# Threshold attention with a SoLU layer behind it: k and q two pairs to a transfer, w_out's copies two pieces at a time, four tiles' swaps issued by GpSimd

## The chip, the core and the metric

The kernel runs on one core of a Trainium2 chip. The core has five engines that run on their own and meet at semaphores: TensorE (PE in the profile, with PEld for its weight loads), VectorE (DVE), ScalarE (ACT), GpSimd (POOL) and SyncE (SP). Transfers are issued by an engine's queue (SPq, ACTq, or GpSimd's) and carried out by 16 DMA engines. The metric is the device time of one execution in microseconds (us); lower is better. Every engine works through its own instructions in order, so an instruction that waits holds all that stand behind it on that engine.

## What is computed

```python
scores = scale * np.matmul(q, k.transpose(0, 1, 3, 2))      # 8 batches, 8 heads, 576 x 576
thresh = np.max(scores, axis=-1, keepdims=True) - tau
scores = np.where(scores >= thresh, scores, -1000000000.0)
attn = np.exp(scores - np.max(scores, axis=-1, keepdims=True))
attn = attn / (np.sum(attn, axis=-1, keepdims=True) + 1e-09)
x = np.matmul(attn, v)                                       # then (B,H,S,D) -> (B*S, H*D)
h = x @ w_in                                                 # 4608 x 512 @ 512 x 1024
e = np.exp(h - h_max)
solu = h * (e / (np.sum(e, axis=-1, keepdims=True) + 1e-09))
ln = (solu - mu) / np.sqrt(var + 1e-06) * g_ln
out = ln @ w_out                                             # 1024 x 512
```

The head dimension is 64, so two heads (a pair) lie beside each other on the 128 partitions. A batch has 4 pairs and 576 tokens.

## The kernel before

**Rounds.** The order of all work is written out by hand. A loop over `rnd` takes one slot (128 score rows of each head of a pair, or left-over rows) per round. A round puts on TensorE the scores of the slot (`scores`, L399) with any transposes of later k and q that are due (`turn_beside`, L344), then a quarter of a feed-forward tile (`ff_h`, L560 and L570, or `ff_o`, L675) or the product with v of an earlier slot (`attend_steps`, L507) or both. VectorE finds each row's threshold (`maxes`, L420), ScalarE applies it and takes exponentials (`ramp` L435, `exps` L444), GpSimd divides by the sums one round later (`normalise`, L451 to L454), and VectorE transposes the result into T (`blocks`, L466).

**T to wT.** After every second slot `blocks` issues on SyncE the copies that regroup T into wT (L475 and L477, three transfers; L482, four, for the left-over rows). L507 needs wT. This is half of all bytes moved.

**Loads of k and q.** Batch 0 comes pair by pair, 128 rows at a time (`load_pair`, L133). Batch 1 comes two pairs at a time (`load_four`, L135 to L142), for k and q of pairs 4 and 5 in rounds 10 and 11, of pairs 6 and 7 in rounds 15 and 16. It puts head e of pair i and head e of pair i + 1 on the two halves of one tile, and issues each half as a transfer of its own, so a call issues four. L344 reads both tiles of a call. Later batches are loaded in another way (`load_natural`, L168) and are transposed by VectorE (L186), with copies of the halves (L188).

**Weights.** w_in and w_out come in 16 pieces of 128 x 512 words of 64 bits, each loaded by SyncE (`weight_load`, L248) and turned into 32 bits by VectorE, ScalarE and GpSimd over two rounds (`weight_e`, `weight_m`, `weight_b`, L258 to L295; `weight_c`, L305). Pieces 8 to 15 are w_out's. For each of them `weight_d` issues two transfers that copy its halves, exchanged, into the odd slots of w2 (L312). `ff_o` reads w2's slots in order, the first eight in its first quarter, and does not run before round and piece counts say that w2 is complete.

**The feed-forward tile.** After `ff_h` a tile's 128 tokens go through `ff_max` (L585), `ff_exp` (L594), `ff_mul` (L600), `ff_sum` (L605), `ff_stats` (L615 to L626), each a round or so apart. Then ScalarE writes the normalised values into V (`ff_norm`, L636), VectorE writes them into u (`ff_norm2`, L641), and `ff_swap` issues four transfers that overwrite quarters of V by rows of u (L652), which exchanges halves. `ff_turn` transposes V into uT (L662), which `ff_o` needs. `ff_norm2` and `ff_swap` stand in the part of the round that the program calls `middle`: behind `normalise` and `weight_c`, ahead of the round's TensorE work in the program's order. Tiles have names of three numbers (batch, kind, m) or one number (the left-over rows of two batches); batch 0 has four of three numbers.

**Queues.** All transfers but two (the first k and half of the last store) are issued by SyncE, in the order of the program.

Of the kernel before, what the change touches and what calls it, by code (L numbers as in the profile page):

```python
# [20 lines left out]
def kernel(  # L21
# [27 lines left out]
    nc = tc.nc  # L49
# [10 lines left out]
    ROWS = (slice(0, 64), slice(64, P))  # L60
# [10 lines left out]
    w2 = const.tile([P, 2 * NC, DM], F32, name="w2")  # L71
# [63 lines left out]
    def load_four(i, nm):  # L135
        heads_of = rows_of[nm][P * i : P * i + 2 * P].rearrange("(j e p) n -> e j p n", j=2, e=2)
        for e in range(2):
            tag = "ends" if nm == "q" and i > NP else nm
            raw = loads.tile([P, NK * D], F32, tag=tag, bufs=BUFS[tag], name=nm)
            whole_rows[i, nm, e] = raw.rearrange("p (m d) -> p m d", m=NK)  # L140
            for j in range(2):
                nc.sync.dma_start(out=raw[ROWS[j]], in_=heads_of[e, j])  # L142

    def load_v(b, hf, parts):
        d = halves.setdefault((b, hf), {})
# [161 lines left out]

    def weight_d(x):
        c = x - 2 * NP
        if c >= 0:  # L310
            for r in range(2):
                nc.sync.dma_start(out=w2[ROWS[r], 2 * c + 1], in_=w2[ROWS[1 - r], 2 * c])  # L312

# [233 lines left out]
    def ff_h(t, part, split, beside=()):  # L549
        beside = iter(beside)  # L550
        x = tokens(t)
        if part == 0:
            tag, h = take("h_ps")
            ffn[t] = dict(h=h, tag=tag, split=split)
        d = ffn[t]
        h = d["h"]
        if not d["split"]:
            f = slice(512 * part, 512 * part + 512)
            for c in range(NP):
                nc.tensor.matmul(  # L560
                    out=h[:, f], lhsT=x[:, c], rhs=w1_parts[:, c, part],
                    start=c == 0, stop=c == NP - 1,
                )
            return
        last = []
        for c in range(NP):
            for r in range(2):
                f = slice(512 * (part ^ r), 512 * (part ^ r) + 512)
                for y in range(2):
                    mm = nc.tensor.matmul(  # L570
                        out=h[ROWS[y], f], lhsT=x[ROWS[r], c, ROWS[y]], rhs=w1_parts[ROWS[r], c, part ^ r],
                        start=part == 0 and c == 0, stop=part == 1 and c == NP - 1,
                    )
                    if part and not last:
                        sync(mm, d["fence"])
                    last.append(mm)
            for _, _ in zip(range(36 * (c > 1)), beside):
                pass
        if part == 0:
            d["fence"] = fence(last[-4:])  # L580

    def ff_max(t):
        d = ffn[t]
        d["nm"] = small.tile([P, 1], F32, tag="hm", name="hm")
        nc.vector.tensor_reduce(out=d["nm"], in_=d["h"], axis=AX.X, op=ALU.max, negate=True)  # L585

    def ff_exp(t):
        d = ffn[t]

        starts.append(t)  # L590
        tag = "xh1" if rnd > NS and len(starts) % 2 else "u"
        d["u"] = work.tile([P, DFF], F32, tag=tag, bufs=1, name="u")
        d["se"] = small.tile([P, 1], F32, tag="se", name="se")
        nc.scalar.activation(  # L594
            out=d["u"], in_=d["h"], func=AF.Exp, bias=d["nm"], scale=1.0, accum_out=d["se"]
        )

    def ff_mul(t):
        d = ffn[t]
        nc.vector.tensor_tensor(out=d["u"], in0=d["h"], in1=d["u"], op=ALU.mult)  # L600
        pairs_free.append(d["tag"])

    def ff_sum(t):
        se = ffn[t]["se"]
        nc.gpsimd.tensor_scalar(out=se, in0=se, scalar1=1e-9, scalar2=None, op0=ALU.add)  # L605
        nc.gpsimd.tensor_tensor(out=se, in0=se, in1=mone[:, 0:1], op=ALU.pow)

    def ff_stats(t):
        d = ffn[t]
        u, se = d["u"], d["se"]  # L610
        bs = small.tile([P, 2, 6], F32, tag="bs", name="bs")
        mv = small.tile([P, 2], F32, tag="mv", name="mv")
        rs = small.tile([P, 1], F32, tag="rs", name="rs")
        for f in range(2):
            nc.vector.bn_stats(out=bs[:, f], in_=u[:, 512 * f : 512 * f + 512])  # L615
        nc.vector.bn_aggr(out=mv, in_=bs)


        nc.gpsimd.tensor_scalar(
            out=rs, in0=mv[:, 1:2], scalar1=se, scalar2=se, op0=ALU.mult, op1=ALU.mult  # L620
        )
        nc.gpsimd.tensor_scalar(out=rs, in0=rs, scalar1=1e-6, scalar2=None, op0=ALU.add)
        nc.gpsimd.tensor_tensor(out=rs, in0=rs, in1=mhalf, op=ALU.pow)
        nc.gpsimd.tensor_tensor(out=rs, in0=rs, in1=se, op=ALU.mult)
        nb = small.tile([P, 1], F32, tag="nb", name="nb")
        nc.gpsimd.tensor_scalar(  # L626
            out=nb, in0=mv[:, 0:1], scalar1=rs, scalar2=-1.0, op0=ALU.mult, op1=ALU.mult
        )
        d["norm"] = rs, nb

    def ff_norm(t):
        d = ffn[t]
        rs, nb = d["norm"]
        d["V"] = V = work.tile([P, 2, DFF // 2], F32, tag="V", bufs=1, name="V")
        u = d["u"].rearrange("p (g n) -> p g n", g=2)
        nc.scalar.activation(out=V, in_=u, func=AF.Identity, bias=nb, scale=rs)  # L636

    def ff_norm2(t):
        d = ffn[t]
        rs, nb = d["norm"]  # L640
        nc.vector.tensor_scalar(  # L641
            out=d["u"], in0=d["u"], scalar1=rs, scalar2=nb, op0=ALU.mult, op1=ALU.add
        )

    def ff_swap(t):
        d = ffn[t]
        for g in range(2):
            for r in range(2):  # L650
                to, of = 64 * r + 32 * g, 64 * r + 32 * (1 - g)
                nc.sync.dma_start(  # L652
                    out=d["V"][to : to + 32, 1 - g],
                    in_=d["u"][of : of + 32, DFF // 2 * g : DFF // 2 * g + DFF // 2],
                )
# [118 lines left out]
    with tc.manual_schedule():  # L774
# [44 lines left out]
        begin, middle, late, norms = {}, {}, {}, {}  # L819
        while True:  # L820
# [10 lines left out]
            if rnd == NS:  # L831
# [4 lines left out]
                if quarter == 2:  # L836
                    between.append(cur)
                    cur = None
                    quarter = 0
                assert quarter != 3  # L840
            if rnd == 13:
                prev, cur, quarter = cur, None, 0
            if (
# [3 lines left out]
                cur = ready[0][1].pop(0)  # L847
# [60 lines left out]
            if step == ("h", 0):  # L908
                ff_h(cur, 0, rnd + 1 < NS, beside)
                quarter = 1  # L910
            elif step == ("h", 1):
                ff_h(cur, 1, None, beside)
                quarter = 2
                by = rnd + 2 * (rnd == 14)
                late.setdefault(by, []).append(lambda t=cur: (ff_max(t), ff_exp(t)))
                late.setdefault(by + 1, []).append(lambda t=cur: (ff_mul(t), ff_sum(t)))
                middle.setdefault(by + 2, []).append(lambda t=cur: ff_stats(t))
                if rnd + 6 < NS:
                    norms[by + 3] = cur
                else:  # L920
                    late.setdefault(rnd + 2, []).append(lambda t=cur: ff_norm(t))
                middle.setdefault(by + 3, []).append(lambda t=cur: (ff_norm2(t), ff_swap(t)))

                at = by + 4 if more or not ready or len(ready[0][1][0]) == 1 else rnd + 6
                if cur == (0, 1, 1):
                    middle.setdefault(rnd + 6, []).append(lambda t=cur, at=rnd + 6: ff_turn(t, at))
                else:
                    late.setdefault(at, []).append(lambda t=cur, at=at: ff_turn(t, at))
                if not more:
                    between.append(cur)  # L930
                    cur = None
                    quarter = 0
            elif step == ("o", 0):
                if prev is not None:
                    ff_o(prev, 0)
                quarter = 3
            elif step == ("o", 1):
                if prev is not None:
                    ff_o(prev, 1)
                    last = not (more or ready or cur or between)  # L940
                    begin.setdefault(rnd + 1, []).append(lambda t=prev, last=last: ff_out(t, last))
                    late.setdefault(rnd + 1, []).append(lambda t=prev, last=last: ff_store(t, last))
                prev, cur = cur, None
                quarter = 0
# [33 lines left out]
            if rnd - 1 in pieces:  # L978
                weight_d(pieces[rnd - 1])
                w2_done = pieces[rnd - 1] == NW - 1  # L980
# [36 lines left out]
```

## Time and profile before

| What | Value |
|---|---|
| Median of 3 runs | 858.18 us (855.24 to 861.62) |
| Profiled execution | 855.96 us |
| Its span, first to last instruction | 854.2 us |
| PE busy | 819.7 us, 96% |
| DVE busy | 680.4 us, 80% |
| ACT busy | 572.3 us, 67% |
| POOL busy | 499.1 us, 58% |
| SyncE's DMA queue | 165.82 MB, packets 77.3% of 16 engines' span |
| Chain that ended last | PE 80%, DVE 7%, DMA 6%, ACT 3% |
| Transfers T to wT | 160 of 288 KB and 64 of 576 KB |
| Swaps V from u | 144 of 64 KB, median 3.4 us to landing |

A group's row in the profile has its source line (L675 is line 675), the engine, the operation, the tile written and the tile read, the number of instructions and their time. In square brackets stand idle time ahead of an instruction and what ended it. A transfer's row on SPq is the time that SyncE needs to issue it; the transfer itself goes on behind that, and the trace records at what time each DMA engine reports its part as landed.

### The profile page before, as it was taken

How to read it: one execution, taken by the hardware profiler on the slowest of the kernel's cores; microseconds unless marked ns; L12 is line 12 of the kernel's file. 1: busy time of each engine (PE TensorE's matmuls, PEld its weight loads, DVE VectorE, ACT ScalarE, POOL GpSimd, SP SyncE). 2: the span in 40 equal slices, each digit the busy share in tenths (PEclk: the TensorE clock that was granted, in tenths of full speed). 3: DMA queues.
4: the chain of work that ended last, by engine and by line, in shares of the span. 5: the costliest groups of instructions: out<-in, count | busy, mean ns of one | idle time of the engine just before them, and what ended most of it. 6: DMA issues, size and time to landing. Idle time of an engine off the chain costs nothing.

```text
span 854.2 us, 36120 instructions
## 1 busy us (share of the span) xinstructions
PE 819.7 (96%) x15363; PEld 613.4 (72%) x15363; DVE 680.4 (80%) x1241; ACT 572.3 (67%) x1127; POOL 499.1 (58%) x945
## 2 busy tenths in 40 slices
PE   6679889999999999999999999999999999999997
PEld 5456666667677787777688877777777777777655
DVE  6999868889788888888788878888888888787361
ACT  6888857877666666666676667766667777775121
POOL 3888637666556656565566666565666655555120
PEclk8889999999999999999999999999999999999999
DMA  9989897898889788887889787888888887655212
GB/s 339 265 236 231 208 206 185 227 250 208 225 208 227 194 191 205 219 214 181 216 212 220 194 177 200 212 212 212 200 207 228 202 195 188 154 136 140 67 39 63
DMA packets 75442, 168.54 MB, mean 197 GB/s; under 512 B 11274, under 2 KB 32786, under 8 KB 75282
## 3 DMA queue, kind: packets, MB, share of 16 engines
q1 hardware_dynamic: 74994, 165.82, 77.3%
q8 instruction: 120, 1.97, 1.0%
q10 hardware_dynamic: 288, 0.43, 0.2%
q14 instruction: 40, 0.33, 0.1%
HBM read 46.14 MB, written 9.44 MB: 65 GB/s over the span
## 4 chain that ended last, share of the span: by engine, by line
PE 80%; DVE 7%; DMA 6%; ACT 3%; issue 2%; POOL 1%; SPq 1%; DVEq 0%; ACTq 0%
PE o_ps L675 27%; PE h_ps L570 21%; PE s_ps L399 15%; PE pv L507 14%; DMA wT<-T 4%; PE h_ps L560 3%; DVE T L466 2%; DVE w L420 2%; ACT w L435 1%; ACT w L444 1%; DVE w L290 1%; DMA V<-u 1%; POOL w L454 0%; PE tp L336 0%; SPq L482 0%
## 5 line engine op out<-in xcount | busy, mean ns | idle before, releaser
L435 ACT ACTIVATE w<-s_ps,nth 128x576 f32<-128x576 f32 x280 | 196.9, 738 | 110.5 <-DVE nth L420 92.0
L675 PE MATMUL o_ps<-w,uT 64*64 64x256 f32 x4608 | 268.4, 376 | 1.3 <-DVE uT L662 0.6
L675 PEld LDWEIGHTS o_ps<-w,uT 64*64 64x64 f32 x4608 | 221.0, 133 | 55.2 <-ACT xh L537 12.0
L420 DVE CUSTOM_DVE_ANT_0 w<-s_ps,tau_t 128x576 f32<-128x576 f32 x280 | 200.1, 751 | 73.7 <-PE s_ps L399 46.3
L454 POOL TENSOR_SCALAR w<-w,sm 128x576 f32<-128x576 f32 x288 | 221.3, 780 | 14.3
L466 DVE STREAM_TRANSPOSE T<-w 128x576 f32<-128x576 f32 x288 | 207.7, 756 | 24.4 <-POOL w L454 23.7
L570 PE MATMUL h_ps<-w,xh 64*64 64x512 f32 x1856 | 220.4, 590 | 0.0
L444 ACT ACTIVATE w<-w,ntau 128x576 f32<-128x576 f32 x288 | 219.5, 766 | 0.0
L507 PEld LDWEIGHTS pv<-wT,v 64*64 64x64 f32 x5760 | 170.4, 135 | 40.7 <-issue 22.9
L399 PE MATMUL s_ps<-kT,qT 64*64 64x64 f32 (+1 forms) x2048 | 173.5, 415 | 16.6 <-ACT w L435 12.5
L507 PE MATMUL pv<-wT,v 64*64 64x128 f32 (+1 forms) x5760 | 173.1, 263 | 7.2 <-DMA wT<-T 5.0
L570 PEld LDWEIGHTS h_ps<-w,xh 64*64 64x64 f32 x1856 | 114.5, 133 | 81.4 <-issue 52.1
L451 POOL TENSOR_SCALAR sm<-sm 128x2 f32<-128x2 f32 x144 | 36.2, 252 | 194.5 <-ACT w L444 191.1
L452 POOL TENSOR_TENSOR sm<-sm,mone 128x2 f32<-128x2 f32 x144 | 108.2, 751 | 12.0
L399 PEld LDWEIGHTS s_ps<-kT,qT 64*64 64x64 f32 x2048 | 70.5, 137 | 25.4 <-ACT w L435 18.0
L537 ACT COPY xh<-pv 128x256 f32<-128x256 f32 x64 | 25.4, 397 | 72.5 <-PE pv L507 72.4
L636 ACT ACTIVATE V<-u,nb,rs 128x1024 f32<-128x1024 f32 x36 | 44.7, 1241 | 41.3 <-POOL nb L626 34.8
L662 DVE STREAM_TRANSPOSE uT<-V 128x1024 f32<-128x1024 f32 x36 | 44.3, 1231 | 21.4 <-DMA V<-u 20.7
L444 ACT ACTIVATION_READ_ACCUMULATOR w<-w,ntau 128x1 f32 x288 | 55.3, 192 | 0.0
L600 DVE TENSOR_TENSOR u<-h_ps,u 128x1024 f32<-128x1024 f32 x36 | 42.8, 1189 | 9.9 <-ACT u L594 9.9
L641 DVE TENSOR_SCALAR u<-u,rs,nb 128x1024 f32<-128x1024 f32 x36 | 34.9, 969 | 17.5 <-ACT V L636 17.4
L594 ACT ACTIVATE u<-h_ps,hm 128x1024 f32<-128x1024 f32 x36 | 40.2, 1117 | 9.9 <-DMA V<-u 5.6
(81 smaller groups left out, 563.7 us busy)
## 6 DMA issues: line engine op xcount, KB each, us to landing
wT<-T SPq DMA_DIRECT2D x160, 288.0 KB, 6.7
wT<-T SPq DMA_DIRECT2D x64, 576.0 KB, 5.5
v<-in_v_dram SPq DMA_DIRECT2D x16, 576.0 KB, 5.7
V<-u SPq DMA_DIRECT2D x144, 64.0 KB, 3.4
out_dram<-ob SPq DMA_DIRECT2D x71, 128.0 KB, 2.6
q<-in_q_dram SPq DMA_DIRECT2D x28, 288.0 KB, 6.0
k<-in_k_dram SPq DMA_DIRECT2D x27, 288.0 KB, 6.5
qT<-flip SPq DMA_DIRECT2D x48, 144.0 KB, 3.5
```

What stands on the lines that cost most here:

```text
L399: nc.tensor.matmul(out=ps[h][ROWS[y], ks], lhsT=lhsT, rhs=d["kT"][ROWS[h], ks], start=True, stop=True,)
L420: nc.vector.tensor_tensor_reduce(out=w, in0=ps[:, 0:S], in1=(zero if loose else tau_t).to_broadcast([P, S]), scale=1.0, scalar=BIG, op0=AL ...
L435: nc.scalar.activation(out=d["w"][x], in_=d["w"][x] if d["loose"] else d["ps"][x][:, 0:S], func=AF.Prelu, bias=d["nth"][x], scale=-1.0, al ...
L444: nc.scalar.activation(out=w, in_=w, func=AF.Exp, bias=ntau, scale=1.0, accum_out=sm[:, x : x + 1])
L452: nc.gpsimd.tensor_tensor(out=sm, in0=sm, in1=mone, op=ALU.pow)
L454: nc.gpsimd.tensor_scalar(out=w, in0=w, scalar1=sm[:, x : x + 1], scalar2=1.0, op0=ALU.mult, op1=ALU.mult)
L466: nc.vector.transpose(out=T[:, :, r, h, :], in_=w)
L507: nc.tensor.matmul(out=to, lhsT=d["v"][ROWS[u], (h0 + h - u) % 4, m,], rhs=rhs, start=m == 0, stop=m == NK - 1,)
L570: mm = nc.tensor.matmul(out=h[ROWS[y], f], lhsT=x[ROWS[r], c, ROWS[y]], rhs=w1_parts[ROWS[r], c, part ^ r], start=part == 0 and c == 0, st ...
L636: nc.scalar.activation(out=V, in_=u, func=AF.Identity, bias=nb, scale=rs)
L662: nc.vector.transpose(out=uT, in_=d["V"].rearrange("p y (m x) -> p m y x", x=32))
L675: nc.tensor.matmul(out=d["o"][ROWS[z], 512 * (r ^ other) : 512 * (r ^ other) + 256], lhsT=d["uT"][ROWS[r], m].rearrange("p y x -> p (y x)" ...
```

## The change

Three edits. `load_four` issues each tile as one transfer, whose source is two blocks of 64 rows. `weight_d` does nothing for an even piece and, for an odd one, copies both pieces' halves in two transfers. `ff_swap` takes the queue that issues it, GpSimd for the four tiles of batch 0 that have three numbers, SyncE for all others. On TensorE, VectorE and ScalarE every instruction stands where it stood.

```diff
@@ load_four
             whole_rows[i, nm, e] = raw.rearrange("p (m d) -> p m d", m=NK)
-            for j in range(2):
-                nc.sync.dma_start(out=raw[ROWS[j]], in_=heads_of[e, j])
+            nc.sync.dma_start(out=raw, in_=heads_of[e])
@@ weight_d
         c = x - 2 * NP
-        if c >= 0:
+        if c > 0 and c % 2:
+            pair_of = w2.rearrange("p (c two) n -> p two c n", two=2)[:, :, c - 1 : c + 1]
             for r in range(2):
-                nc.sync.dma_start(out=w2[ROWS[r], 2 * c + 1], in_=w2[ROWS[1 - r], 2 * c])
+                nc.sync.dma_start(out=pair_of[ROWS[r], 1], in_=pair_of[ROWS[1 - r], 0])
@@ ff_swap
-    def ff_swap(t):
+    def ff_swap(t, queue):
         d = ffn[t]
         for g in range(2):
             for r in range(2):
                 to, of = 64 * r + 32 * g, 64 * r + 32 * (1 - g)
-                nc.sync.dma_start(
+                queue.dma_start(
@@ the loop over rounds
-                middle.setdefault(by + 3, []).append(lambda t=cur: (ff_norm2(t), ff_swap(t)))
+                middle.setdefault(by + 3, []).append(lambda t=cur: (ff_norm2(t), ff_swap(t, nc.gpsimd if t[0] < 1 and len(t) > 1 else nc.sync)))
```

## The prediction

> **What bounds the kernel now.** All times are us. First the page's slices (each 21.4): TensorE (PE) is full from the seventh slice on, and the DMA engines are nearly full early.
>
> ```profile
> PE   6679889999999999999999999999999999999997
> DMA  9989897898889788887889787888888887655212
> ```
>
> So a delay caused early is not won back later, and time can be won only before about 130. Next, busy time by stretch (engine busy us with instruction counts, granted clock, share of the 16 DMA engines, GB/s):
>
> ```profile
> 10.00:18.00 8.00, 4.75 (x108) 3.38 (x107) 6.83 (x17) 7.75 (x16) 4.03 (x6) 0.90 1.04 403
> 20.00:30.00 10.00, 7.59 (x109) 5.60 (x107) 9.90 (x23) 8.85 (x17) 8.29 (x10) 0.67 1.03 265
> 66.00:140.00 74.00, 68.56 (x1397) 48.72 (x1393) 62.58 (x122) 56.09 (x114) 50.18 (x87) 1.00 0.85 208
> ```
>
> From 66 to 140, where every edit lies, PE idles 74 - 68.56 = 5.4. The DMA engines are 85% busy there. Rows one and two price one engine: 403 / 16 / 1.04 = 24.2 GB/s with loads from HBM alone, 265 / 16 / 1.03 = 16.1 GB/s with loads and copies mixed. The issues by line (KB each, median from issue to landing), and SyncE's queue (SPq) in order of time:
>
> ```profile
> k<-in_k_dram SPq DMA_DIRECT2D x8, 144.0 KB, 3.4
> q<-in_q_dram SPq DMA_DIRECT2D x8, 144.0 KB, 4.4
> w<-w SPq DMA_DIRECT2D x16, 128.0 KB, 4.6
> 69.01 2.52 SPq L142 DMA_DIRECT2D k<-in_k_dram  x4
> 74.35 2.52 SPq L142 DMA_DIRECT2D q<-in_q_dram  x4
> 76.97 0.60 SPq L475 DMA_DIRECT2D wT<-T  x1
> 96.48 2.52 SPq L142 DMA_DIRECT2D k<-in_k_dram  x4
> 99.11 0.61 SPq L475 DMA_DIRECT2D wT<-T  x1
> 102.24 3.40 SPq L142 DMA_DIRECT2D q<-in_q_dram  x4
> 113.91 4.56 SPq L652 DMA_DIRECT2D V<-u  x4
> ```
>
> Each issue holds SPq about 0.6. Behind each k and q group stands a wT transfer. PE, which works in order, shows when these are wanted:
>
> ```profile
> 78.61 1.45 PE L344 MATMUL s_ps<-ident,k 64*64 64x64 f32 x50
> 84.98 0.28 PE L344 MATMUL s_ps<-ident,q 64*64 64x64 f32 x2
> 86.83 2.66 PE L507 MATMUL pv<-wT,v 64*64 64x128 f32 x72
> 93.33 0.44 PE L507 MATMUL pv<-wT,v 64*64 64x128 f32 x4 [0.62 <-DMA wT<-T]
> 105.88 1.48 PE L344 MATMUL s_ps<-ident,k 64*64 64x64 f32 x50
> 108.17 2.19 PE L507 MATMUL pv<-wT,v 64*64 64x128 f32 x70
> 110.95 0.27 PE L344 MATMUL s_ps<-ident,q 64*64 64x64 f32 x2
> ```
>
> By the landing records these k groups are complete at 74.7 and 102.2, the q groups at 82.1 and 108.5: 2.5 to 4 before PE wants them. Last, VectorE (DVE):
>
> ```profile
> 122.41 1.25 DVE L662 STREAM_TRANSPOSE uT<-V 128x1024 f32<-128x1024 f32 x1 [4.91 <-DMA V<-u]
> ```
>
> This is the largest wait for a transfer that the change touches.
>
> **The loads of k and q.** Sixteen transfers of 144 KB become eight of 288 KB: eight issues less, 8 x 0.6 = 4.8 of SPq. The new source is no longer 64 rows but [2, 64, 576]: two blocks of 64 rows, 128 rows apart, so the leading count is 2; the target is 128 rows. How many engines share such a transfer, no row of before shows. Nearest are the landing records, one from each engine: the one-row load of tau has 1, the eight-row load of g_rows 8 (14.21 to 15.44), every transfer with 32, 64 or 128 leading rows 16; where engines are missing, one record more comes at once (0.47 after g_rows' issue). So engines are given shares of the leading dimension, or of all rows: the two readings agree on every row of before. I take the leading dimension, as no transfer there shows engines split below it, and put 2 engines in each new load.
>
> The Trainium skill, "DMA: Bandwidth & Descriptors", section "Why a DMA increments its semaphore by 16 and not by 1", says that the count is the largest number up to 16 that divides both sides' slowest dimension that isn't 1, and that on SyncE's queue it is the lowest-numbered engines; the trace agrees with 1, 8 and 16, and no row shows a 2. By it the sum is the one that follows; by all rows it would be rival B's.
>
> With 2 engines each carries 147.5 KB a load: 147.5 / 24.2 = 6.1, at the other end 147.5 / 16.1 = 9.2. I take 6.1, since these are loads from HBM and the other engines run dry meanwhile. All other SPq transfers have a share on these two engines and wait there in order: a wT group (1,180 KB / 16 = 73.7 KB) takes 73.7 / 16.1 = 4.6, the 512 KB weight 1.4, a pair of w_out copies 2.0. D is PE's delay so far.
> - k: the engines are free at 70.9 (the wT before has landed); 70.9 + 12.2 = 83.1, wanted 78.6: D = 4.5. The weight lands at 84.5 where DVE's L258 at 79.9 wants it: the same 4.6.
> - q: 84.5 + 2.0 + 12.2 = 98.7, wanted 85.0 + 4.5: D = 13.7.
> - wT: 103.3, wanted 86.8 + 13.7: D = 16.5. Next wT: 103.3 + 2.0 + 4.6 = 109.9, wanted 93.3 + 16.5: in time.
> - k again: 122.1, wanted 105.9 + 16.5: in time. wT: 126.7, wanted 108.2 + 16.5: D = 18.5.
> - q again: 138.9, wanted 111.0 + 18.5: D = 28.
> Within the last stall DVE's 4.91 for V passes, and with it PE's idle pieces from 89 to 98 and 122 to 128, together 4.8, of which I credit 4: **+24**. With 9.2 the same steps give 10.7, 26.1, 28.9, 28.9, 34.8, 37.1, 52.8, less 4: +49. As the low end I take half of +24, if SyncE's earlier issues and other work done in the stalls hide the rest.
>
> **The copies of w_out.** Sixteen of 128 KB become eight of 256 KB, 64 leading rows as before: 8 x 0.6 = 4.8 of SPq, same bytes. An even piece's copy waits a round for the odd one. Its first reader is L675 at 97.97; the last copies of before are issued at 95.25 and land at 98.2, and they serve the second half of that product, 102.42. Cover 4.2 for a pair that lands perhaps 1 later: 0. Without that cover it costs that 1.
>
> **The swaps on GpSimd (POOL).** Sixteen issues leave SPq, 16 x 0.6 = 9.6. They stand behind normalise's L454 and wait there for DVE's L641; behind them are the next round's L451 to L454, for which DVE's L466 waits, and behind that wT. No row shows a POOL issue. Bounds: POOL's shortest arithmetic 0.2, SPq's longest swap issue 1.9, so 0.8 to 7.6 a tile; I take SPq's median 0.6, the same work, 2.4. Tile 1: POOL idles 0.95 at 91.6, so about 1.5 late. Tile 2: L641 ends 111.75, POOL idles to 114.11, so 0. Tiles 3 and 4: 2 and 1 late, against PE without idle time. With 7.6 a tile it is 6.6, 0, 7 and 6. Against this stands up to 4.7 of the 4.91 at tile 2 (rival B). Net between -4.7 and +20; I take 0, because the stalls above cover tiles 1 and 2 and the median row is the nearest.
>
> **Sum.** +24 + 0 + 0. The profiled execution is 855.96 (span 854.2 and 1.76 around it), which becomes 880; it lies 2.2 below the median of 858.18, on which I forecast **882**. In this case alone: 870 to 907.
>
> **Rivals.** One per cent, about what a measurement can tell, is 8.6.
> - A, the forecast, two engines carry the loads: 0.76 (of it 0.03 under 8.6).
> - B, the other side: engines share all 128 rows. Then the loads cost nothing, and one mechanism decides: the swap of tile 2 leaves POOL at 111.75 instead of SPq at 113.91 to 118.5 behind the v loads. Four issues (2.4) and 3.4 to land (the median of V<-u) end at 117.6 instead of 122.33. Its price is capped by PE's idle 5.4; I take -4: 854. It decides if the loads' landing records are 16. For it: DVE's 4.91. Against: the leading 1 and 8. Chance 0.15, a third of it past 1% if more of SPq's 19.2 counts.
> - The Trainium skill, same page, "Rules for kernel authors", advises one 128-partition transfer in place of two to disjoint halves; by it B would be the outcome, and no run here shows it.
> - C: 16 engines, but POOL's issues are near 1.9 and hold normalise: of the 20 a third reaches PE, the rest goes into DVE's own idle time: +6, 864. For it: L466 waits for L454 already. Chance 0.09, a third of it beyond 1%.
>
> **Numbers.** Slower: 0.73 + 0.03 = 0.76; same 0.03 + 0.10 + 0.06 = 0.19; faster 0.05. The range 856 to 907 takes in A's bounds and all of C; it leaves out B's better part and a tail of A past +49, some 0.17.
>
> **What would show it.** A: three landing records on each new load (two engines and one at once), 12 or more from issue to the second's landing, L344 waiting for k and q, L507 for wT, some 24 more PE idle between 75 and 140, nothing changed after. B: 16 records, landings near 6, L662's wait gone. C: L466 waiting for L454. I am wrong if the loads are spread, or if PE's queue has work that covers the two q waits.

## The result, and the profile after

| | before | changed |
|---|---|---|
| Median of 6 runs each, us | 859.02 (855.24 to 863.95) | 894.84 (893.78 to 899.39) |
| Ratio, 95% interval | | 1.0428 [1.0382, 1.0473] |
| Profiled execution (span), us | 855.96 (854.2) | 894.05 (892.3) |
| PE busy; span less busy, us | 819.7; 34.5 | 829.5; 62.8 |

Times are in us, differences are of medians, and one run of the kernel before that stands beside e5 to e8 (866.09) was in a slower state of the chip and is left out of its median.

The changed kernel is slower by 35.8. Between the profiled executions it is 38.1: PE idles 28.3 longer and is busy 9.8 longer, although it runs the same instructions. The changed kernel's profiled execution was some 2.2 behind before the first new load: the wT transfer that SyncE issues at 63.34 in the kernel before comes at 65.55, after 10.2 of half clock on PE (52.2 to 62.4) where the kernel before has 3.4 (54.0 to 57.4). In nine of the ten runs below, with any part of the change, that transfer comes at 62.9 to 64.4, so most of this lag belongs to the one execution.

The slices of the changed kernel (each 22.3 wide; PEclk is the granted clock of PE in tenths):

```profile
PE   6679484999999999999999999999999999999997
PEclk8869696999999999999999999999999999999999
DMA  9984736689888887898788878888788877655312
```

The DMA engines, nearly full there before, drop to between 30 and 80% in slices 4 to 8 (67 to 178). PE drops to 40% in slices 5 and 7 (89 to 112 and 134 to 156), and its clock with it. From slice 8 on PE is full, as before. By stretches (columns as in the prediction: engine busy with counts, granted clock, DMA share, GB/s):

```profile
66.00:140.00 74.00, 52.62 (x966) 39.65 (x958) 44.93 (x86) 41.95 (x85) 41.73 (x70) 0.85 0.55 137
100.00:110.00 10.00, 4.40 (x72) 3.75 (x76) 0.76 (x2) 0.00 (x0) 0.00 (x0) 0.50 0.65 158
148.90:154.60 5.70, 5.70 (x66) 4.14 (x70) 2.06 (x7) 1.20 (x3) 0.00 (x0) 0.50 0.42 108
```

From 66 to 140 PE's busy time falls from 68.56 to 52.62, and the transfers from 208 GB/s to 137. The chip was short of neither work nor bandwidth: ACT and POOL did nothing at all between 100 and 110, and the transfers wanted next stood in a queue. SyncE's queue shows what held it:

```profile
76.97 8.57 SPq L141 DMA_DIRECT2D q<-in_q_dram  x2
85.67 5.44 SPq L475 DMA_DIRECT2D wT<-T  x1
...
121.32 6.52 SPq L141 DMA_DIRECT2D q<-in_q_dram  x2
```

Two loads where there were four take 8.57 and 6.52 to issue instead of 2.52 and 3.40, and a single wT transfer 5.44 instead of 0.6. (The change takes one line out of `load_four`, so L142 is now L141, the load, and L248 is now L247, the weight's; from L312 on the numbers are as before.) The landing records say which engines are meant. For the second k load, the second q load and the wT transfer that follows it in the queue, the times at which engines report their parts:

```
issue    tile  records
70.26    k     71.5, 85.99, 86.66
77.67    q     85.96, 104.87, 105.56
85.67    wT    94.67, 94.77, 94.8, 94.83, 94.86, 94.88, 94.89, 94.9, 95.0, 95.03, 95.11, 95.33, 95.84, 95.95, 106.28, 106.97
```

Each of the eight loads has three records, one at once and two late. The wT transfer is complete on 14 engines at 95.95; the two that carry q come 11.0 later, and L507 cannot start before the last. PE's list shows the same loads from the other side:

```profile
86.70 1.49 PE L344 MATMUL s_ps<-ident,k 64*64 64x64 f32 x48 [2.21 <-DMA k<-in_k_dram]
96.10 0.33 PE L344 MATMUL s_ps<-ident,q 64*64 64x64 f32 x2 [2.31 <-DMA q<-in_q_dram]
105.60 1.71 PE L344 MATMUL s_ps<-ident,q 64*64 64x64 f32 x32 [9.18 <-DMA q<-in_q_dram]
130.09 1.49 PE L344 MATMUL s_ps<-ident,k 64*64 64x64 f32 x48 [0.19 <-DMA k<-in_k_dram]
139.51 0.47 PE L344 MATMUL s_ps<-ident,q 64*64 64x64 f32 x2 [4.16 <-DMA q<-in_q_dram]
148.90 1.71 PE L344 MATMUL s_ps<-ident,q 64*64 64x64 f32 x32 [8.91 <-DMA q<-in_q_dram]
```

Each of these starts within 0.05 of a landing. Before, k stood at 78.61 and 105.88, and the bulk of the second group's q at 111.17:

```profile
111.17 0.82 PE L344 MATMUL s_ps<-ident,q 64*64 64x64 f32 x28
```

So the delay is 8.1 at the first k, 24.2 at the second and 37.7 at the last q, and 38.1 at the end. Nearly all of it is made by 149. The chain of waits has two q loads as its longest pieces in this part (start, us, what):

```profile
77.67 27.89 DMA q<-in_q_dram
...
121.92 26.94 DMA q<-in_q_dram
```

### The profile page after: what moved, and what is told of

Read it like the earlier page. It is cut to its first block, busy times and chain, and to the rows that moved or that the text cites. A ratio compares the mean times of both kernels' runs of the same rounds, so it can differ in the third digit from the quotient of the medians.

```text
span 892.3 us, 36114 instructions
## 1 busy us (share of the span) xinstructions
PE 829.5 (93%) x15363; PEld 624.8 (70%) x15363; DVE 680.3 (76%) x1241; ACT 573.5 (64%) x1127; POOL 507.9 (57%) x961
## 3 DMA queue, kind: packets, MB, share of 16 engines
q1 hardware_dynamic: 73858, 164.77, 73.7%
## 4 chain that ended last, share of the span: by engine, by line
PE 79%; DMA 11%; ACT 3%; DVE 2%; POOL 2%; issue 2%; SPq 1%; ACTq 0%; POOLq 0%; DVEq 0%
PE o_ps L675 26%; PE h_ps L570 21%; PE s_ps L399 15%; PE pv L507 14%; DMA q<-in_q_dram 6%; DMA wT<-T 4%; PE h_ps L560 3%; ACT w L435 1%; ACT w L444 1%; DVE w L420 1%; DMA raw<-in_moe_w_in_dram 1%; POOL w L454 1%; PE s_ps L344 1%; POOL sm L452 0%; DVE T L466 0%
## 5 line engine op out<-in xcount | busy, mean ns | idle before, releaser
L675 PE MATMUL o_ps<-w,uT 64*64 64x256 f32 x4608 | 272.2, 378 | 2.6 <-DVE uT L662 1.7
L675 PEld LDWEIGHTS o_ps<-w,uT 64*64 64x64 f32 x4608 | 220.3, 134 | 59.1 <-ACT xh L537 10.5
L454 POOL TENSOR_SCALAR w<-w,sm 128x576 f32<-128x576 f32 x288 | 221.8, 782 | 14.4
L466 DVE STREAM_TRANSPOSE T<-w 128x576 f32<-128x576 f32 x288 | 207.6, 755 | 23.2 <-POOL w L454 22.5
L507 PEld LDWEIGHTS pv<-wT,v 64*64 64x64 f32 x5760 | 175.2, 137 | 39.8 <-issue 19.7
L399 PE MATMUL s_ps<-kT,qT 64*64 64x64 f32 (+1 forms) x2048 | 178.5, 419 | 15.6 <-ACT w L435 12.4
L507 PE MATMUL pv<-wT,v 64*64 64x128 f32 (+1 forms) x5760 | 177.8, 265 | 6.8 <-DMA wT<-T 5.5
L570 PEld LDWEIGHTS h_ps<-w,xh 64*64 64x64 f32 x1856 | 119.3, 134 | 78.0 <-issue 41.1
L399 PEld LDWEIGHTS s_ps<-kT,qT 64*64 64x64 f32 x2048 | 74.8, 139 | 24.3 <-ACT w L435 17.3
L662 DVE STREAM_TRANSPOSE uT<-V 128x1024 f32<-128x1024 f32 x36 | 44.3, 1229 | 19.3 <-DMA V<-u 19.2
L641 DVE TENSOR_SCALAR u<-u,rs,nb 128x1024 f32<-128x1024 f32 x36 | 34.5, 959 | 17.8 <-ACT V L636 17.8
```

Source lines behind the costliest of these rows:

```text
L399: nc.tensor.matmul(out=ps[h][ROWS[y], ks], lhsT=lhsT, rhs=d["kT"][ROWS[h], ks], start=True, stop=True,)
L454: nc.gpsimd.tensor_scalar(out=w, in0=w, scalar1=sm[:, x : x + 1], scalar2=1.0, op0=ALU.mult, op1=ALU.mult)
L466: nc.vector.transpose(out=T[:, :, r, h, :], in_=w)
L507: nc.tensor.matmul(out=to, lhsT=d["v"][ROWS[u], (h0 + h - u) % 4, m,], rhs=rhs, start=m == 0, stop=m == NK - 1,)
L570: mm = nc.tensor.matmul(out=h[ROWS[y], f], lhsT=x[ROWS[r], c, ROWS[y]], rhs=w1_parts[ROWS[r], c, part ^ r], start=part == 0 and c == 0, st ...
L662: nc.vector.transpose(out=uT, in_=d["V"].rearrange("p y (m x) -> p m y x", x=32))
```

## The experiments

The theory (A) is the forecast's: each new load is on two engines, and all that follows in the queue waits for those two. The runs are called e1 to e10. The rivals are costs of the other two edits, a fixed cost of the new form whatever the number of engines, loads that are only late in the queue, and the order on SyncE's queue alone. Every ratio is to runs of the kernel before on the same chip.

**The parts alone.** First only the loads are changed, then only the copies and the swaps, then only the swaps.

```diff
# e1_loads_only: of the change, load_four alone
-            for j in range(2):
-                nc.sync.dma_start(out=raw[ROWS[j]], in_=heads_of[e, j])
+            nc.sync.dma_start(out=raw, in_=heads_of[e])
# e2_rest_only: weight_d and ff_swap alone; e8_pool_only: ff_swap alone
```

> The kernel before with the loads' edit alone (eight loads of 288 KB whose source leads with 2). Theory A (two engines carry each load): nearly the whole loss is here, 30 to 42 us over the kernel before, three landing records on each load. Rival (the swaps on GpSimd or the paired copies make the loss, for instance by holding normalise): under 10 us.

> The change without the loads' edit: paired copies of w_out and four swaps on GpSimd. Theory A: between 6 us faster and 4 us slower than before; the wait of L662 for V near 120 us shrinks from 4.9 to under 2. Rival (the swaps hold GpSimd's normalise): 10 us or more slower, with L466 waiting for L454.

> The kernel before with the four swaps on GpSimd alone. The prediction's sum: 0 net, 4 us faster to 6 us slower; L662's wait near 120 us under 2, L466's waits for L454 some 3 to 7 us more in total. Rival (the swaps gain 4 and the paired copies lose them): 3 to 5 us faster.

The loads alone: 894.22 against 857.74, 1.0418 [1.0389, 1.0446], or +36.5, with three landing records on each load. The rest alone: 859.08, 1.0002 [0.9974, 1.003]. The swaps alone: 858.4, 1.0019 [0.9991, 1.0047]. So the whole loss is the loads', and SyncE's 9.6 + 4.8 of issue time that the other two edits free are worth nothing here that the runs could tell from zero. What became of the wait at L662 can be read in the timeline of the run without the loads:

```profile
113.43 2.12 POOL L652 DMA_DIRECT2D V<-u  x4 [2.02 <-ACT w L435]
...
117.53 1.50 DVE L466 STREAM_TRANSPOSE T<-w 128x576 f32<-128x576 f32 x2 [1.29 <-POOL w L454]
...
120.40 1.25 DVE L662 STREAM_TRANSPOSE uT<-V 128x1024 f32<-128x1024 f32 x1 [1.37 <-DMA V<-u]
```

The wait for V shrinks from 4.91 to 1.37, as rival B had it. But POOL itself stands still for 2.02 ahead of its four issues and takes 2.12 for them, and L466 waits 1.29 behind L454. Over the whole run, its waits (us in total, times, longest) have

```profile
DVE T L466 <- POOL w L454: 30.0, 28, 2.6
```

where the kernel before has 23.7 in all and the run with the swaps alone 25.7. And L662's waits for V over the whole run are 20.8, against 20.7 before: what is saved at this tile comes back at later ones. So DVE has gained nothing. That this is why the time stays the same is read from the traces; no run separates it.

**The number of engines.** The whole change, but with the source of each load cut into 16 blocks of 8 rows, or four of 32, instead of two of 64: the same bytes in the same transfers, but other rows of k and q in the tile, so the output is no longer the attention that the kernel should compute. These two runs are for the time alone.

```diff
-        heads_of = rows_of[nm][P * i : P * i + 2 * P].rearrange("(j e p) n -> e j p n", j=2, e=2)
+        heads_of = rows_of[nm][P * i : P * i + 2 * P].rearrange("(j e p) n -> e j p n", j=16, e=2)   # e3_blocks16
+        heads_of = rows_of[nm][P * i : P * i + 2 * P].rearrange("(j e p) n -> e j p n", j=4, e=2)    # e4_blocks4
```

> The whole change, but each load of two pairs takes 16 blocks of 8 rows in place of two blocks of 64, the same bytes and issues (so k and q of batch 1 have their rows in another order and the output is another one). Theory A (the source's leading count sets the number of engines): 16 landing records, the loss gone, as the kernel without the loads' edit to within 3 us. Rival (all 128 rows count, and something else of a single 128-partition load is slow): 3 records or a loss of 30 us and more stays.

> As the kernel with 16 blocks, with four blocks of 32 rows. Theory A: four engines, five landing records, a load takes 3 to 5 us on them, and by the prediction's steps with 3.05 in place of 6.1 the delay is about 4 us: 0 to 10 us over the kernel with 16 blocks. Rival (any source of several blocks is slow): as slow as the change, 30 us and more.

With 16 blocks each load has 16 records and the time is 859.62, 1.0018 [1.0, 1.0037]: the loss is gone, with every other thing of the change in place. With four there are five records and 872.25, 1.0165 [1.013, 1.02]. From 66 to 140 of the run with 16 and, below it, of the run with four:

```profile
66.00:140.00 74.00, 68.12 (x1380) 46.15 (x1376) 62.58 (x123) 55.46 (x114) 53.79 (x95) 0.98 0.87 207
```

```profile
66.00:140.00 74.00, 57.91 (x1044) 41.73 (x1039) 50.04 (x97) 44.89 (x91) 44.66 (x76) 0.91 0.74 174
```

The first is the kernel before again (68.56, 0.85, 208); the second lies between it and the change. This rules out a fixed cost of the form, since e3 has the same eight issues and bytes: over e2, which has no new loads, it is +35.8 for 2 engines, +13.2 for 4 and +0.5 for 16. The miss is in e4's size, +12.6 over e3 where at most 10 was expected. That bound came from the prediction's rate, 73.7 KB / 24.2 = 3.05 a load; on the slowest engine the landings of the two loads of a call were 5.3, 3.2, 3.2 and 5.2 apart, 4.2 on the mean. The prediction's steps with 4.2 give 12.7, and 8.7 when its credit of 4 is taken off.

**One tensor alone.** The loads of k only, then of q only, as single transfers; all else as before.

```diff
-            for j in range(2):
-                nc.sync.dma_start(out=raw[ROWS[j]], in_=heads_of[e, j])
+            for j in range(1 if nm == "k" else 2):      # e6_q_only: "q", here and in the next line
+                nc.sync.dma_start(**(dict(out=raw, in_=heads_of[e]) if nm == "k" else dict(out=raw[ROWS[j]], in_=heads_of[e, j])))
```

> The kernel before, with k's four loads alone as one transfer of two blocks (two engines), q's as before. The prediction's table, with 7.6 us a load as the changed kernel's landings show: k stops the PE by 7.7, wT by 1 more, the second k by 3, its wT by 2: 14, less about 2 of idle time: 10 to 16 us over before. Rival (every two-engine load costs a fixed 37 / 8 = 4.6 us): 18.

> The kernel before, with q's four loads alone on two engines. The same table with 7.6 us: q 8, wT 3, the second q 7 to 8: 18, less 2 to 4: 12 to 18 us over before. With k alone the sum is 22 to 34, below the 37 of both, as a k group in front delays the q group behind it. Rival (a fixed 4.6 us a load): 18, and the two add up to 37.

Against 856.95 for the kernel before beside them: k 872.66, 1.0174 [1.0147, 1.0202], +15.7; q 873.1, 1.0188 [1.016, 1.0217], +16.1. Both as the theory had it; a fixed price for each load would give half of e1's 36.5, 18.2, which lies outside k's interval (it ends at +17.3) and inside q's (+18.6). Together 31.8 is less than 36.5. By the steps of the prediction that is to be expected, since loads that are followed by ordinary transfers find some slack and q loads behind k loads find none; how much of the 4.7 comes from that was not measured.

**Earlier.** If the loads were only late, calling them five to seven rounds earlier should hide them. Of the change this run has the loads alone.

```diff
-    for i, at, nm in ((NP, 10, "k"), (NP, 11, "q"), (NP + 2, 15, "k"), (NP + 2, 16, "q")):
+    for i, at, nm in ((NP, 4, "k"), (NP, 6, "q"), (NP + 2, 8, "k"), (NP + 2, 10, "q")):
```

> The loads' edit alone, with the four calls moved from rounds 10, 11, 15, 16 to 4, 6, 8, 10, so that k and q are asked for 4 rounds and more before PE wants them. Theory A (engines 0 and 1 lack the throughput, and everything behind waits in order): the wait moves to the weights, wT and v that stand behind, 20 us or more over before. Rival (the loads only come too late): under 8 us over before.

899.11, 1.0493 [1.0461, 1.0524], +42.2. The rival falls. In PE's list L344 no longer waits for the loads, and L507 waits for wT instead:

```profile
65.24 0.69 PE L507 MATMUL pv<-wT,v 64*64 64x128 f32 x4 [10.97 <-DMA wT<-T]
85.50 0.69 PE L507 MATMUL pv<-wT,v 64*64 64x128 f32 x4 [14.62 <-DMA wT<-T]
104.20 4.70 PE L507 MATMUL pv<-wT,v 64*64 64x128 f32 x70 [5.11 <-DMA wT<-T]
```

Moving the loads moves the stall to what stands behind them, as it must when the two engines are what is short.

**Another queue.** Of the change the loads alone; the eight are issued by ScalarE, or by GpSimd, so that wT does not stand behind them on SyncE's queue.

```diff
+            nc.scalar.dma_start(out=raw, in_=heads_of[e])      # e9_act_loads
+            nc.gpsimd.dma_start(out=raw, in_=heads_of[e])      # e10_gp_loads
```

> The loads' edit alone, with the eight loads issued by ScalarE, whose queue is not the one that wT, weights and copies stand in. Theory A, as throughput (eight loads of 7.6 us lie on two engines that had some 11 us free between 66 and 140): the loss stays, 25 to 45 us over before, with ScalarE held in its issues as SyncE was (6 to 8 us twice). Rival (only the order behind the loads in one queue costs, engines take turns between queues): under 12 us over before.

> The same with the eight loads issued by GpSimd. Theory A: if GpSimd's two-engine transfers lie on the same two engines each time, 25 to 45 us over before; if each takes other engines, a load still needs about 7 us and lands in time or up to 5 us late, nothing queues up behind eight of them: 0 to 10 us over before. The Trainium skill, DMA: Bandwidth & Descriptors, section Why a DMA increments its semaphore by 16 and not by 1, says that GpSimd's transfers take their engines in turn; by it the second.

From ScalarE: 900.18, 1.0473 [1.0433, 1.0512], +42.2, so the loss does not need the order on SyncE's queue. Its waits on PE, and the worst place of ACT's own list:

```profile
PE s_ps L344 <- DMA q<-in_q_dram: 21.7, 3, 8.0
PE pv L507 <- DMA wT<-T: 3.6, 4, 2.4
```

```profile
72.75 10.56 ACTq L141 DMA_DIRECT2D q<-in_q_dram  x2
...
83.42 1.37 ACT L435 ACTIVATE w<-s_ps,nth 128x576 f32<-128x576 f32 x2 [9.95 <-issue]
```

The first wT transfers after the q loads land 8.8 to 10.2 after their issue instead of 15.8 to 21.3, but the first q loads land at 96.84 and 106.19, no earlier than from SyncE (96.05 and 105.56). The size is confounded: of the 10.56 in the list ACT is held for 4.72 and 2.35 in the two issues, with 3.49 between them, and its exponentials stand behind them. The run shows that the two engines are slow from this queue too, not how much of the +42 is theirs.

From GpSimd: 876.31, 1.0184 [1.0134, 1.0235], +18.3, which is neither of the two outcomes expected. The waits:

```profile
PE s_ps L344 <- DMA k<-in_k_dram: 3.9, 1, 3.9
PE pv L507 <- DMA wT<-T: 8.4, 7, 3.9
```

Each load now has 16 records, but lands only 15.8 to 25.8 after its issue. The records of the packets show why: 512 packets of 4,608 bytes at some 0.32 each, and from 107.1 to 127.1 256 of them, so 256 x 0.32 / 20 = 4.1 engines at work on the mean. That is more than two and far fewer than 16. Nor do 16 records mean 16 engines here: in either group of four loads, the first has 2 records that come late (119.43 and 120.60, where the other 14 are in by 109.66), the second 4, the third 6 and the fourth 8. That is what two engines a load leave, each load on two others, when every engine reports behind the work that it has. The Trainium skill, "DMA: Bandwidth & Descriptors", section "Why a DMA increments its semaphore by 16 and not by 1", says that on GpSimd's queue all 16 engines report whatever the shape, and that a transfer with fewer engines takes consecutive ones in turn instead of the lowest-numbered; the 16 records and the 2, 4, 6 and 8 late ones agree with that. By these records the expectation's second case came in its mechanism, but not in its price: a load does not need about 7. The packets of wT, of the same size, take as long beside them (0.317 on the mean from 107.1 to 127.1, the loads' 0.315). Why a load takes this form here stays open, and so does what POOL's 0.8 to 1.0 for each issue adds.

Not tried: tiles of 128 consecutive rows, which need another order in the transposes, and tiles of 64 partitions by two, which by e3's count should have 16 engines, with half the issues. With e2 and e3 equal to the kernel before, fewer issues have nothing to win here; no version that beats it was found.

## Why the prediction was right, and where its sizes were off

**Two engines.** Right. The reading that engines are given shares of the leading dimension (2, not 128 rows) decided the sign; three records, and e3 and e4, show it. The rule of the Trainium skill named in the prediction now has rows for 2, 4 and 16, with 3, 5 and 16 records. The advice from the same page (section "Rules for kernel authors") to use one 128-partition transfer in place of two halves takes it that both run on all 16 engines. The source here leads with 2, and in e1 joining the halves makes the kernel 1.0418 times as long.

**"I take 6.1".** The mis-sized term. On the slower of the two engines the landings were 7.1, 6.4, 6.8, 9.5, 8.0, 7.2, 6.6 and 9.4 apart: 61.0 / 8 = 7.6, between the two ends 6.1 and 9.2. The reason given for the low end, that the other engines run dry meanwhile, was true (DMA share 0.55), but it did not give these two the rate of HBM loads alone all the time. An engine moves its half of a load in 64 packets of 2,304 bytes. Those that started from 80.27 to 86.66, while the second k load moved with few other packets about, took 106 ns on the mean (median 96, which would be 6.1 a load); from 96.05 to 105.56, while the second q load moved beside copies within SBUF, 165. With 7.6 in place of 6.1 the prediction's own steps give 7.5 at k, 19.7 at q, 22.5 at wT, 25.2 at the next k, 27.5 at wT and 39.9 at the last q, less the credit of 4: +35.9. Measured were 8.1 at k, 24.2 at the next k, 37.7 at the last q, and +35.8 in the medians. The agreement is one of steps with a size that was read afterwards, and its closeness is in part luck: 2.2 of the measured delays were there before the first new load, and the credit of 4 is not seen. In e1, without those 2.2, the landings are 7.2 apart on the mean; the steps with 7.2 give 36.7 at the last q before the credit, and there it is 36.5 late (147.65 for 111.17), the loss of its median too:

```profile
147.65 1.71 PE L344 MATMUL s_ps<-ident,q 64*64 64x64 f32 x32 [8.26 <-DMA q<-in_q_dram]
```

In e4 the same correction was needed (4.2 for 3.05), and again the steps fit without the credit (12.7 for 12.6) and not with it (8.7).

**Every transfer with a share on the two engines waits.** Right: the records of wT show it, and with the loads early (e7) PE waits 32.2 for wT in all and no longer for k and q. What the steps did not have is that SyncE itself is held in an issue, up to 7.88; no run separates what that costs.

**Where PE waits.** L344 for k and q, the last of them until 148.9, and for no load later: as forecast, but for the end, which was put at 140. L507's waits for wT are not: they total 5.5 over the run against 5.0 before. In the steps they were +2.8 and +2.0. The first is there as a delay, since L507 runs at 108.98 where it ran at 86.83 (+22.2, by the steps with 7.6 +22.5). But it is not seen as a wait for wT, since L344 and L399 work from 105.60 to 108.98 while wT lands at 108.43. "Some 24 more PE idle" came out as 28.3, and 9.8 of slower work was not foreseen: after the first new load PE's clock stood at 0.5 for 34.1, where the kernel before has none of it. Work that is slower ahead of a wait for the next load only shortens that wait. The stretch after the last load is different: 5.70 of work at half clock (148.9 to 154.6, shown above). From the last q load to the end PE is busy 1.5 longer than before (733.28 and 731.77) and idle 1.1 shorter (10.0 and 11.2). These 1.1 are all that the trace shows of the credit, and the delay grows by 0.4, from 37.7 to 38.1. That account is read from one trace, not tested by a run.

**Copies and swaps at zero.** Right: 1.0002 and 1.0019. A POOL issue takes 0.5 (median 506 ns), 2.0 a tile where 2.4 was taken. Rival B's mechanism is there at its tile (4.91 to 1.37), and rival C's too (L466 behind L454). That the two cancel is a reading; what is shown is that neither decides, as the interval of e2 leaves at most 2.6 either way.

## What to carry to other kernels

Before joining two transfers into one, look at the outermost dimension of both sides: here two blocks of 64 rows put 288 KB on two of 16 engines, and the saving of eight issues of 0.6 cost 36. For a transfer on SyncE's or ScalarE's queue the landing records tell it at a glance (on GpSimd's, e10 had 16 records for loads that moved on few engines). A queue served in order passes such a delay to every transfer behind it, so that the wait may show at another tile than the one that causes it. Price a busy engine by its rate under the traffic that stays beside it, and keep both ends where that is not known.

## What the runs showed of the hardware that was not expected

- **Half clock after idling.** PE's granted clock went to 0.5 at 96.6 to 110.2, 120.4 to 123.9 and 137.5 to 154.6. In the 3.4 ahead of each stretch PE had been busy for only 0.77, 1.56 and 1.25, and each ended 3.8 to 5.7 after PE had taken up work again (105.60, 120.04, 148.90). 64 matmuls of L675 took 5.37 mostly within the second of these stretches, where the first 64 of the kernel before took 3.68. In PE's list of the kernel before and, below it, of the changed kernel:

```profile
97.97 3.68 PE L675 MATMUL o_ps<-w,uT 64*64 64x256 f32 x64 [0.58 <-DVE uT L662]
```

```profile
120.04 5.37 PE L675 MATMUL o_ps<-w,uT 64*64 64x256 f32 x64 [1.65 <-DVE uT L662]
```

  Long stalls and time at half clock go together: after the first new load's time it is 34.1 in the changed kernel and in e1, 13.7 in e4, 3.4 in e3 and none in e2. But e8, which has no new loads and no loss in its median, has 6.8, so a few us of it say nothing by themselves. The stretches are 3.4, 13.6 and 17.1 long, multiples of 3.4. The Trainium skill, "TensorE: Matmul & The Clock Gate", Part 1 on the HAM clock gate, has the clock throttled by default and released by some 3.4 us of activity; these lengths, and work of 3.8 to 5.7 before each release, agree.
- **An issue can hold its engine.** SyncE stood 7.88 and 5.92 in the second q load of a pair, ACT 4.72 in one (e9), against 0.6 for an ordinary issue.
- **GpSimd's form of the same load.** 16 records instead of 3, of which two more come late with each load of a group, packets of 4,608 bytes, about four engines at work on the mean, 15.8 to 25.8 to landing.
